# Moving 256 rows of a weight matrix out of the main loads of a one-token attention and gMLP layer

## The chip, the cores and the metric

The kernel runs on one core of one Trainium2 chip. A core has a matrix engine (TensorE, PE in the profile), VectorE (DVE), ScalarE (ACT), GpSimd (POOL) and SyncE (SP), which run their own queues of instructions and wait for each other by semaphores, and 16 DMA engines. The metric is the device time of one execution, in microseconds (us).

## The reference

One token with 576 features is normalised and goes through two branches, whose results are added to it. Branch A is attention over the last 4096 positions of a cache with 16 heads for 32 query heads. Branch B is a gated MLP with 2304 pairs of hidden values.

```python
xn = layernorm(x)                                        # x: [1, 1, 576]
q = (xn @ wq).reshape(1, 1, 32, 128).transpose(0, 2, 1, 3)
k = repeat(k_cache[:, :, 65536 - 4096:, :], 2, axis=1)   # v the same
p = softmax(einsum('bhqd,bhkd->bhqk', q, k) * 128 ** -0.5)
A = einsum('bhqk,bhkd->bhqd', p, v).transpose(0, 2, 1, 3).reshape(1, 1, 4096) @ wo

z = gelu(xn @ w_in)                                      # w_in: [576, 4608]
z1, z2 = z[..., :2304], layernorm(z[..., 2304:])
g = w_sp * z2 + b_sp                                     # one position: two numbers
B = (z1 * g) @ w_out                                     # w_out: [2304, 576]
out = x + A + B
```

All inputs and the output are bfloat16. Some 51 MB are read for one token.

## The kernel before

**Loads.** Nearly all data comes in by DMAs that SyncE issues in a fixed order, near the top of the kernel: wq in two pieces, k blocks 0 and 1, v block 0, then k2, v1, k3, w_in (win), v2, v3, wo in two pieces and w_out (wout) in four. Each fills all 128 partitions of a tile. A block holds four of the 16 cache heads. The tiles come from two pools of two buffers each, "small" and "large", so a load waits until the tile that was in its buffer two turns earlier is used up: wo waits for the z matmuls that read win, and wout for the transposes of k block 3. The scheduler is manual: the program text sets each engine's order, and a framework adds the semaphore waits that its view of the tiles asks for.

**Attention.** For each block b, `turn` (L211) transposes k on VectorE, `scores` (L251) makes the scores on PE and their softmax on VectorE and ScalarE (the exponential p at L279), `weigh` (L287) multiplies by v into pv, which ScalarE copies to pvs (L298), and `heads` (L301) reduces that to eight columns of o_t. `values` is heads after weigh.

**The MLP.** `z_all` (L319) multiplies xn by win on PE (L329), nine steps deep, into two tiles z0 and z1. VectorE copies them into zs (L333 to L336), whose last part GpSimd has set to zero (L321), and transposes zs in 32x32 blocks into zt (L337, L338), so that the hidden values stand on the partitions. `gate` (L341) makes the gelu, the layer norm and the product: a chain of small steps on VectorE with an exponential (L351) and the norm's Ln and Exp (L181, L182) on ScalarE and a sum over the partitions on PE (L362). It ends with hv (L369), the column that multiplies w_out.

**Rows of w_out.** 2304 rows are 18 for each of 128 partitions. In the kernel before, the main load brings 17 rows a partition (FR = 17), rows 128 to 2303. The first 128 rows are the "side rows": two DMAs that ScalarE issues (L382, L383), ahead of its exponential of block 3, bring 96 of them to 12 partitions of eight rows each, and 32 to 32 partitions of one row each. The z values that belong to the side rows are picked from z0 by two small copies (L334, L336), and hv has FC = 26 columns.

**The end.** `row_of` (L392) adds one row of each partition to the result: two matmuls, one for each half of the 576 outputs. PE's order there is: the sum of the gate's layer norm (L362), heads(2), the input row, the side rows, values(3), a transpose of o_t into o_p, 32 rows of wo, and 17 rows of wout; then two copies of the result and two DMAs to the output. The cuts (0, 8, 14, 16, 17) of the main load of w_out let PE begin with its first rows while the rest is on the way.

Of the kernel before, what the change touches and what calls it, by code (L numbers as in the profile page):

```python
# [8 lines left out]
FP32 = mybir.dt.float32  # L9
# [5 lines left out]
P = 128  # L15
D = 576
# [5 lines left out]
FH = 2304  # L22
# [6 lines left out]
NR = 9  # L29
EPS = 1e-5  # L30
SCALE = DH ** -0.5
GELU_C = 0.7978845608028654
FE = P
FR = (FH - FE) // P
FX = 8
FB = 12 * FX
FC = FR + FX + 1
FQ = P * FR // 4
FW = FQ // 2
WR = HQ * DH // P  # L40
HW = D // 2
ZPAD = 24
# [6 lines left out]
def kernel(  # L49
# [14 lines left out]
    nc = tc.nc  # L64
    ctx.enter_context(tc.manual_schedule())

    const = ctx.enter_context(tc.tile_pool(name="const", bufs=1))
    work = ctx.enter_context(tc.tile_pool(name="work", bufs=2))
    one = ctx.enter_context(tc.tile_pool(name="one", bufs=1))
# [7 lines left out]
    ps_a = ctx.enter_context(tc.tile_pool(name="ps_a", bufs=2, space=PS))  # L77


    x_row = const.tile([1, D], BF16, name="x_row")  # L80
    nc.scalar.dma_start(x_row[:], A_x.flatten_outer_dims())
    ws2 = const.tile([1, 2], BF16, name="ws2")
    nc.scalar.dma_start(ws2[:, 0:1], B_w_sp.flatten_outer_dims()[0:1, 0:1])
    nc.scalar.dma_start(ws2[:, 1:2], B_b_sp.flatten_outer_dims()[0:1, 0:1])
# [3 lines left out]
    def unit(name, width):  # L88
        pool = small if width == SMALL else large
        return pool.tile([P, width], BF16, name=name, tag="u")  # L90
# [4 lines left out]
    def load(t, view, width, cuts):  # L95
        for a, e in zip(cuts, cuts[1:]):
            nc.sync.dma_start(t[:, (a - cuts[0]) * width:(e - cuts[0]) * width], view[:, a * width:e * width])
# [19 lines left out]
    win_t = unit("win", LARGE)  # L117
# [3 lines left out]
    wo_t = unit("wo", LARGE)  # L121
    load(wo_t, wo_v, D, (0, 20, WR))
    wout_t = unit("wout", SMALL)
    load(wout_t, B_w_out[FE:FH, :].rearrange("(p r) n -> p (r n)", r=FR), D, (0, 8, 14, 16, FR))


    ident = const.tile([P, P], BF16, name="ident")
# [1 line left out]
    xw = const.tile([P, NR, 32], BF16, name="xw")  # L129
# [91 lines left out]
    for r in range(NR):  # L221
        for g in range(4):
            nc.tensor.matmul(q_ps[32 * g:32 * g + 32, :], lhsT=xw[:, r, :],  # L223
                             rhs=wq_t[:, 2048 * r + 512 * g:2048 * r + 512 * (g + 1)],
                             start=r == 0, stop=r == NR - 1, tile_position=(0, 32 * g))
# [5 lines left out]
    for g in range(4):  # L231
        nc.tensor.matmul(qr[:, :, g, :], lhsT=rep4[:, g, :, :].rearrange("p n q -> p (n q)"),
                         rhs=qT[:, :, 0:2, :].rearrange("p a h e -> p h a e"), start=True, stop=True)
# [17 lines left out]
    def scores(b):  # L251
        sm = one.tile([P, 2, 512], FP32, name=f"sm{b}", tag="sm")
        mx = work.tile([P, 2], FP32, name=f"mx{b}", tag="mx")
        for kk in range(2):
            s_ps = ps_s.tile([P, 512], FP32, name=f"s{b}_{kk}", tag="s")
            for k4 in range(4):
                for ce in range(4):
                    c, e = divmod(ce, 2)
                    nc.tensor.matmul(s_ps[:], lhsT=zq[:, b, ce, ZPAD - 8 * k4:ZPAD - 8 * k4 + P],  # L259
                                     rhs=kt[b, 4 * kk + k4][:, c, :, e],  # L260
                                     start=k4 == 0 and ce == 0, stop=k4 == 3 and ce == 3)
            nc.vector.tensor_tensor_reduce(  # L262
                out=sm[:, kk, :].rearrange("p (n s) -> p n s", s=HB),
                in0=s_ps[:].rearrange("p (n s) -> p n s", s=HB),
                in1=cm[:].unsqueeze(1).to_broadcast([P, P, HB]), scale=SCALE, scalar=-3e38,
                op0=ALU.add, op1=ALU.max, accum_out=mx[:, kk:kk + 1])
        m1 = work.tile([P, 1], FP32, name=f"m1{b}", tag="m1")
        nc.vector.tensor_max(m1[:], mx[:, 0:1], mx[:, 1:2])  # L268
        tr = ps_m.tile([P, P], FP32, name=f"tr{b}", tag="m")
        nc.tensor.matmul(tr[:], lhsT=m1[:].to_broadcast([P, P]), rhs=ident_f[:], start=True, stop=True)  # L270
        m8 = work.tile([P, 8], FP32, name=f"m8{b}", tag="m8")
        nc.vector.tensor_reduce(out=m8[:], in_=tr[:].rearrange("p (a x) -> p x a", x=8), axis=AXX, op=ALU.max)  # L272
        mj = work.tile([P, 8], FP32, name=f"mj{b}", tag="mj")
        nm = work.tile([P, 1], FP32, name=f"nm{b}", tag="nm")
        nc.vector.tensor_tensor_reduce(out=mj[:], in0=m8[:], in1=sel8[:], scale=-1.0, scalar=0.0,  # L275
                                       op0=ALU.mult, op1=ALU.add, accum_out=nm[:])
        p = one.tile([P, 1024], BF16, name=f"p{b}", tag="p")
        l = work.tile([P, 1], FP32, name=f"l{b}", tag="l")
        nc.scalar.activation(p[:], sm[:].rearrange("p k n -> p (k n)"), ACT.Exp, bias=nm[:], accum_out=l[:])  # L279
        p_t[b] = work.tile([P, 2, 16, 32], BF16, name=f"pt{b}", tag="pt")  # L280
        nc.vector.transpose(p_t[b][:].rearrange("p k u m -> p (k u m)"), p[:])  # L281
        su = ps_m.tile([P, 8], FP32, name=f"su{b}", tag="m")
        nc.tensor.matmul(su[:], lhsT=l[:].to_broadcast([P, P]), rhs=sel8[:], start=True, stop=True)  # L283
        rms[b] = work.tile([P, 8], FP32, name=f"rm{b}", tag="rm")
        nc.vector.reciprocal(rms[b][:], su[:])
# [23 lines left out]
    def values(b):  # L309
        heads(b, weigh(b))  # L310


    hv = const.tile([P, FC], BF16, name="hv")

    zt = const.tile([P, FC, 32], FP32, name="zt")
    nc.gpsimd.memset(zt[:, FR:, :], 0.0)


    def z_all():  # L319
        zs = one.tile([P, FQ + 32 * (FX + 1)], FP32, name="zs", tag="sm")  # L320
        nc.gpsimd.memset(zs[0:32, FQ:], 0.0)  # L321
        zx = zs[0:32, FQ:].rearrange("p (r i) -> p r i", i=32)
        zp = [ps_a.tile([P, FE + FW], FP32, name=f"z{i}", tag="a") for i in range(2)]
        for r in range(NR):
            for g in range(4):
                for i in range(2):
                    lead = FE if g == 0 and i == 0 else 0
                    a = FE + FQ * g + FW * i - lead
                    nc.tensor.matmul(zp[i][32 * g:32 * g + 32, FE - lead:], lhsT=xw[:, r, :],  # L329
                                     rhs=win_t[:, FH * r + a:FH * r + a + lead + FW],  # L330
                                     start=r == 0, stop=r == NR - 1, tile_position=(0, 32 * g))
        for i in range(2):
            nc.vector.tensor_copy(zs[:, FW * i:FW * (i + 1)], zp[i][:, FE:])  # L333
        nc.vector.tensor_copy(zx[:, 0:FX, 0:12].rearrange("p r (i x) -> p r i x", x=4),  # L334
                              zp[0][0:32, 0:FB].rearrange("p (x i r) -> p r i x", x=4, i=3))
        nc.vector.tensor_copy(zx[:, FX, :], zp[0][0:32, FB:FE])  # L336
        nc.vector.transpose(zt[:, 0:FR, :], zs[:, 0:FQ].rearrange("p (i r) -> p r i", r=FR))  # L337
        nc.vector.transpose(zt[0:32, FR:, :], zx)  # L338
        return zt[:, :, 0:2]

    def gate(z):  # L341
        def t3(name):
            return const.tile([P, FC, 2], FP32, name=name)

# [8 lines left out]
        nc.vector.reciprocal(e[:], e[:])  # L353
        G = const.tile([P, 2, FC], FP32, name="G")
        nc.vector.tensor_mul(G[:].rearrange("p h c -> p c h"), e[:], z)
        sz = const.tile([P, 2], FP32, name="sz")
        nc.vector.tensor_reduce(out=sz[:, 0:1], in_=G[:, 1, :], axis=AXX, op=ALU.add)
        jz = const.tile([P, FC], FP32, name="jz")
        nc.vector.tensor_tensor_reduce(out=jz[:], in0=G[:, 1, :], in1=G[:, 1, :], scale=1.0, scalar=0.0,
# [3 lines left out]
        mz = rstd_of(sp[:], FH, "mz")  # L363
        gz = const.tile([P, FC], FP32, name="gz")
        nc.vector.tensor_scalar(out=gz[:], in0=G[:, 1, :], scalar1=mz[:, 0:1], scalar2=mz[:, 3:4],
# [12 lines left out]
    values(1)  # L378
    turn(3)

    e0 = D * (FR + FX)
    nc.scalar.dma_start(wout_t[0:12, D * FR:e0], B_w_out[0:FB, :].rearrange("(x i r) n -> i x (r n)", x=4, i=3))  # L382
    nc.scalar.dma_start(wout_t[0:32, e0:e0 + D], B_w_out[FB:FE, :])  # L383
    scores(3)
    z = z_all()
    pvs2 = weigh(2)
    gate(z)
# [4 lines left out]
    def row_of(col, w, start=False, stop=False):  # L392
        for g in range(2):
            nc.tensor.matmul(fin[g][32 * g:32 * g + 1, :], lhsT=col, rhs=w[:, HW * g:HW * (g + 1)],  # L394
                             start=start, stop=stop, tile_position=(0, 32 * g))

    row_of(one_bf[:, 0:1], x_row, start=True)
    for r, rows in [(FR + j, 12) for j in range(FX)] + [(FR + FX, 32)]:
        row_of(hv[0:rows, r:r + 1], wout_t[0:rows, D * r:D * (r + 1)])
    values(3)  # L400


# [48 lines left out]
```

## Time and profile before

| | |
|---|---|
| median of three runs | 127.53 us (127.42 to 127.91) |
| the profiled execution's own time | 127.4 us |
| its span, from the first to the last instruction | 125.6 us |
| mean granted clock of TensorE | 0.864 |
| TensorE busy | 77.5 us (62%) |
| VectorE busy | 64.7 us (52%) |
| ScalarE busy | 10.2 us |
| GpSimd busy | 4.5 us |
| bytes moved by DMA | 51.03 MB, mean 406 GB/s |

Busy times are the time in which the profiler saw an instruction of the engine at work, as a share of the span. In a line of the timeline stand the start, the busy time, the engine, the line of the kernel, the operation, what it writes and reads with shapes, and the number of instructions; in brackets behind it how long the engine had been idle and what ended that. ACTq and SPq are the queues in which ScalarE and SyncE issue DMAs: such a line gives the time of the issue, not of the transfer. The "chain that ended last" follows the work back from the last instruction, at each step to what released it. Durations in ns are of one instruction.

The DMA engines were busy almost throughout: in 40 equal slices of the span their mean busy share was 0.8 or more in all but the first and the last.

### The profile page before, as it was taken

What the parts mean: (1) busy time and instruction counts of PE and PEld (TensorE: products, weight loads), DVE (VectorE), ACT (ScalarE), POOL (GpSimd) and SP (SyncE); (2) the same over time, 40 slices, a digit from 0 to 9 for tenths busy, and PEclk for the clock granted to TensorE, in tenths of its full rate; (3) what the DMA queues carried; (4) which work ended last, traced back from release to release, by engine and by line L of the source; (5) the groups of instructions that cost most, each with busy time, mean ns of one, the idle gap of its engine ahead of it and who ended that gap; (6) DMA issues with size and microseconds to landing.
All of it is one profiled execution on the core that took longest, in us unless ns stands there. A gap on an engine that the chain in (4) does not pass through costs nothing.

```text
span 125.6 us, 1352 instructions
## 1 busy us (share of the span) xinstructions
PE 77.5 (62%) x546; PEld 37.7 (30%) x550; DVE 64.7 (52%) x132; ACT 10.2 (8%) x19; POOL 4.5 (4%) x12
## 2 busy tenths in 40 slices
PE   3230550099922997385799274997397188749661
PEld 3110220033302342225334033342274063235340
DVE  6660032499648998322998445998326840010001
ACT  4010000000021000310000221000300210100001
POOL 8500000000000000000000000000100000000000
PEclk9999999999985599955579999599958975786999
DMA  4999899898998979999898999989898989999960
GB/s 120 506 438 438 365 470 470 365 501 365 470 459 378 485 344 490 407 428 490 355 490 365 508 423 428 423 384 490 358 462 372 487 359 444 448 395 423 396 249 0
DMA packets 2526, 51.03 MB, mean 406 GB/s; under 512 B 298, under 2 KB 461, under 8 KB 717
## 3 DMA queue, kind: packets, MB, share of 16 engines
q1 hardware_dynamic: 2450, 50.81, 94.9%
q10 hardware_dynamic: 71, 0.15, 0.3%
q8 instruction: 4, 0.07, 0.2%
q14 instruction: 1, 0.01, 0.0%
HBM read 50.96 MB, written 0.00 MB: 406 GB/s over the span
## 4 chain that ended last, share of the span: by engine, by line
PE 42%; DMA 37%; DVE 11%; ACT 5%; issue 2%; SPq 1%; ACTq 0%
PE s L259 29%; DMA wout<-in_B_w_out_dram 20%; DMA k<-in_A_k_cache_dram 18%; ACT p L279 4%; PE pv L293 4%; DVE kt L214 4%; PE z L329 4%; PE op L304 2%; DVE sm L262 2%; PE tr L270 2%; PE fin L394 1%; DVE pt L281 1%; DVE m L272 1%; ACT pvs L298 1%; PE su L283 1%
## 5 line engine op out<-in xcount | busy, mean ns | idle before, releaser
L259 PE MATMUL s<-kt,zq 128*128 128x512 bf16 x124 | 36.3, 451 | 11.6 <-DVE kt L214 10.8
L214 DVE STREAM_TRANSPOSE kt<-k 128x1024 f32<-128x1024 f32 x32 | 36.4, 1204 | 3.9 <-DMA k<-in_A_k_cache_dram 3.9
L259 PEld LDWEIGHTS <-zq 128*128 128x128 bf16 x128 | 14.5, 113 | 32.4 <-issue 21.4
L293 PE MATMUL pv<-v,pt 128*32 128x512 bf16 x128 | 10.1, 469 | 1.1 <-DMA v<-in_A_v_cache_dram 1.1
L279 ACT ACTIVATE p<-sm,nm 128x1024 bf16<-128x1024 f32 x4 | 4.6, 1148 | 71.9 <-DVE nm L275 71.9
L223 PE MATMUL q_ps<-wq,xw 128*32 128x512 bf16 x36 | 4.2, 627 | 7.2 <-DMA wq<-in_A_wq_dram 4.9
L307 DVE TENSOR_TENSOR o_t<-op,rm 128x8 bf16<-128x8 f32 x4 | 0.7, 164 | 15.1 <-PE op L304 15.1
L281 DVE STREAM_TRANSPOSE pt<-p 128x1024 bf16<-128x1024 bf16 x4 | 5.0, 1245 | 5.4 <-ACT p L279 5.4
L262 DVE CUSTOM_DVE_ANT_1 sm<-s,cm 128x512 f32<-128x512 f32 x8 | 5.4, 671 | 3.5 <-PE s L259 3.5
L304 PE MATMUL op<-selu,pvs 128*128 128x8 f32 x32 | 5.3, 293 | 2.5 <-ACT pvs L298 2.1
L283 PE MATMUL su<-sel,l 128*128 128x8 f32 x8 | 1.8, 293 | 7.6 <-ACT p L279 7.6
L394 PE MATMUL fin<-wo,o_p 128*1 128x288 bf16 x64 | 5.7, 345 | 1.2 <-DMA wo<-in_A_wo_dram 1.1
L304 PEld LDWEIGHTS op<-selu,pvs 128*128 128x128 f32 x32 | 5.0, 236 | 4.6 <-ACT pvs L298 4.2
L418 DVE CAST res<-fin 1x288 bf16<-1x288 f32 x1 | 0.4, 445 | 11.4 <-PE fin L394 11.4
L394 PE MATMUL fin<-wout,hv 128*1 128x288 bf16 (+2 forms) x52 | 4.8, 336 | 2.3 <-DMA wout<-in_B_w_out_dram 2.2
L293 PEld LDWEIGHTS <-pt 128*32 128x32 bf16 x128 | 3.7, 112 | 5.8 <-issue 3.1
L227 DVE CAST q_sb<-q_ps 128x512 bf16<-128x512 f32 x1 | 0.7, 690 | 8.1 <-PE q_ps L223 8.1
L394 PEld LDWEIGHTS <-o_p 128*1 128x1 bf16 x64 | 3.3, 99 | 4.0 <-issue 1.1
L329 PE MATMUL z<-win,xw 128*32 128x272 bf16 (+1 forms) x72 | 4.4, 396 | 0.0
L270 PE MATMUL tr<-ident_f,m 128*128 128x128 f32 x8 | 2.0, 326 | 3.9 <-DVE m L268 3.9
L223 PEld LDWEIGHTS <-xw 128*32 128x32 bf16 x36 | 1.4, 130 | 9.2 <-issue 9.2
L298 ACT COPY pvs<-pv 128x512 f32<-128x512 f32 x4 | 2.3, 585 | 20.2 <-PE pv L293 20.2
(93 smaller groups left out, 41.8 us busy)
## 6 DMA issues: line engine op xcount, KB each, us to landing
k<-in_A_k_cache_dram SPq DMA_DIRECT2D x4, 4096.0 KB
v<-in_A_v_cache_dram SPq DMA_DIRECT2D x4, 4096.0 KB, 29.2
win<-in_B_w_in_dram SPq DMA_DIRECT2D x1, 5184.0 KB
wq<-in_A_wq_dram SPq DMA_DIRECT2D x1, 3584.0 KB, 12.7
wo<-in_A_wo_dram SPq DMA_DIRECT2D x1, 2880.0 KB
wo<-in_A_wo_dram SPq DMA_DIRECT2D x1, 1728.0 KB, 20.8
wout<-in_B_w_out_dram SPq DMA_DIRECT2D x1, 1152.0 KB
wq<-in_A_wq_dram SPq DMA_DIRECT2D x1, 1024.0 KB, 4.7
```

What stands on the lines that cost most here:

```text
L214: nc.vector.transpose(t[:].rearrange("p c n e -> p (c n e)").bitcast(FP32), kn[b][:, UK * DH * k:UK * DH * (k + 1)].bitcast(FP32).rearrang ...
L223: nc.tensor.matmul(q_ps[32 * g:32 * g + 32, :], lhsT=xw[:, r, :], rhs=wq_t[:, 2048 * r + 512 * g:2048 * r + 512 * (g + 1)], start=r == 0, ...
L259: nc.tensor.matmul(s_ps[:], lhsT=zq[:, b, ce, ZPAD - 8 * k4:ZPAD - 8 * k4 + P], rhs=kt[b, 4 * kk + k4][:, c, :, e], start=k4 == 0 and ce = ...
L262: nc.vector.tensor_tensor_reduce(out=sm[:, kk, :].rearrange("p (n s) -> p n s", s=HB), in0=s_ps[:].rearrange("p (n s) -> p n s", s=HB), in ...
L270: nc.tensor.matmul(tr[:], lhsT=m1[:].to_broadcast([P, P]), rhs=ident_f[:], start=True, stop=True)
L279: nc.scalar.activation(p[:], sm[:].rearrange("p k n -> p (k n)"), ACT.Exp, bias=nm[:], accum_out=l[:])
L281: nc.vector.transpose(p_t[b][:].rearrange("p k u m -> p (k u m)"), p[:])
L293: nc.tensor.matmul(pv[32 * g:32 * g + 32, :].rearrange("p (n d) -> p n d", n=4), lhsT=p_t[b][:, kk, u, :], rhs=v4[:, kk, u, :, :], start=k ...
L298: nc.scalar.copy(pvs[:], pv[:])
L304: nc.tensor.matmul(op[:], lhsT=pvs[:, DH * u:DH * (u + 1)], rhs=selu[:, 8 * u:8 * u + 8], start=u == 0, stop=u == 3)
L329: nc.tensor.matmul(zp[i][32 * g:32 * g + 32, FE - lead:], lhsT=xw[:, r, :], rhs=win_t[:, FH * r + a:FH * r + a + lead + FW], start=r == 0, ...
L394: nc.tensor.matmul(fin[g][32 * g:32 * g + 1, :], lhsT=col, rhs=w[:, HW * g:HW * (g + 1)], start=start, stop=stop, tile_position=(0, 32 * g))
```

## The change

The main load of w_out brings 16 rows a partition instead of 17, in the cuts (0, 8, 13, 15, 16), and 256 rows are side rows. The first 96 of these are brought by ScalarE as before to 12 partitions of eight rows each, but the DMA stands behind scores(3), and so behind the exponential of block 3, in ScalarE's queue. The other 160 are brought by a DMA of GpSimd to the partitions 64 to 79, ten rows each. Ahead of it GpSimd sets the side rows' part of the wout tile to zero (10 columns of rows on 128 partitions), and before and after the block's DMA it issues a small copy, `skip`, of 16 numbers twice for eight and for four partitions, each fourth of the first 32, into columns of the tile that nothing reads. All four stand ahead of the memset of zs on GpSimd.

In z_all the products change shape: per step four of 512 columns into z0, and two, of 96 and 160 columns, into z1, so 54 matmuls instead of 72. zs, zt and hv have 16 + 10 columns. The side rows are ten products over all 128 partitions (the zeros add nothing) instead of nine over 12 or 32. The input row x is loaded in two halves instead of one piece.

```diff
-FE = P
-FR = (FH - FE) // P
-FX = 8
-FB = 12 * FX
-FC = FR + FX + 1
...
+FR = 16
+FA, RA = 96, 8
+FB, RB = 160, 10
+FE = FA + FB
+FC = FR + RB
+FQ = 512
...
-    nc.scalar.dma_start(x_row[:], A_x.flatten_outer_dims())
+    for a in range(0, D, D // 2):
+        nc.scalar.dma_start(x_row[:, a:a + D // 2], A_x.flatten_outer_dims()[:, a:a + D // 2])
...
-    load(wout_t, B_w_out[FE:FH, :].rearrange("(p r) n -> p (r n)", r=FR), D, (0, 8, 14, 16, FR))
+    load(wout_t, B_w_out[FE:FH, :].rearrange("(p r) n -> p (r n)", r=FR), D, (0, 8, 13, 15, FR))
...
-    zt = const.tile([P, FC, 32], FP32, name="zt")
-    nc.gpsimd.memset(zt[:, FR:, :], 0.0)
...
+        zs = one.tile([P, FQ + 32 * RB], FP32, name="zs", tag="sm")
+        nc.gpsimd.memset(zs[:, FQ:], 0.0)
+        zx = zs[:, FQ:].rearrange("p (r i) -> p r i", i=32)
...
         for r in range(NR):
             for g in range(4):
...
+                product(0, g, r, FE + FQ * g, FQ, 0)
+            product(1, 0, r, 0, FA, 0)
+            product(1, 2, r, FA, FB, FA)
+        nc.vector.tensor_copy(zs[:, 0:FQ], zp[0][:])
+        for q, n, a, rows, k in ((0, 12, 0, RA, 3), (64, 16, FA, RB, 4)):
+            nc.vector.tensor_copy(
+                zx[q:q + 32, 0:rows, 0:n].rearrange("p r (i x) -> p r i x", x=4),
+                zp[1][q:q + 32, a:a + n * rows].rearrange("p (x i r) -> p r i x", x=4, i=k))
+        zt = one.tile([P, FC, 32], FP32, name="zt", tag="zt")
         nc.vector.transpose(zt[:, 0:FR, :], zs[:, 0:FQ].rearrange("p (i r) -> p r i", r=FR))
-        nc.vector.transpose(zt[0:32, FR:, :], zx)
+        nc.vector.transpose(zt[:, FR:, :], zx)
...
-    e0 = D * (FR + FX)
-    nc.scalar.dma_start(wout_t[0:12, D * FR:e0], B_w_out[0:FB, :].rearrange("(x i r) n -> i x (r n)", x=4, i=3))
-    nc.scalar.dma_start(wout_t[0:32, e0:e0 + D], B_w_out[FB:FE, :])
+    def blocks(a, e, k):
+        return B_w_out[a:e, :].rearrange("(x i r) n -> i x (r n)", x=4, i=k)
+
+    def skip(k, a):
+        nc.gpsimd.dma_start(wout_t[0:4 * k:4, a:a + 32].rearrange("i (m c) -> i m c", m=2),
+                            B_w_out[0:2 * k, 0:16].rearrange("(m i) n -> i m n", m=2))
+
+    nc.gpsimd.memset(wout_t[:, D * FR:D * FC], 0.0)
+    skip(8, D * FC)
+    nc.gpsimd.dma_start(wout_t[64:80, D * FR:D * FC], blocks(FA, FE, 4))
+    skip(4, D * FC + 32)
     scores(3)
+    nc.scalar.dma_start(wout_t[0:12, D * FR:D * (FR + RA)], blocks(0, FA, 3))
     z = z_all()
...
-    for r, rows in [(FR + j, 12) for j in range(FX)] + [(FR + FX, 32)]:
-        row_of(hv[0:rows, r:r + 1], wout_t[0:rows, D * r:D * (r + 1)])
+    for r in range(FR, FC):
+        row_of(hv[:, r:r + 1], wout_t[:, D * r:D * (r + 1)])
```

In the changed kernel's own line numbers, which the prediction uses for it, skip is L388, GpSimd's memset of wout L391 and its block L393, ScalarE's side rows L396, the memset of zs L318, the copies of the side rows' z L334, their transpose L339, and the gate's sum L363. The other names of lines are those of the kernel before.

More of the change, by code (lines that the diff above doesn't have):

```diff
@@ L32 @@
 GELU_C = 0.7978845608028654
-FE = P
-FR = (FH - FE) // P
-FX = 8
-FB = 12 * FX
-FC = FR + FX + 1
-FQ = P * FR // 4
-FW = FQ // 2
+FR = 16
[4 more added lines that the diff above has]
+FQ = 512
 WR = HQ * DH // P
@@ L313 @@
     hv = const.tile([P, FC], BF16, name="hv")
-    zt = const.tile([P, FC, 32], FP32, name="zt")
-    nc.gpsimd.memset(zt[:, FR:, :], 0.0)
     def z_all():
[L320 to L323, printed above, removed]
+        zs = one.tile([P, FQ + 32 * RB], FP32, name="zs", tag="sm")
+        nc.gpsimd.memset(zs[:, FQ:], 0.0)
@@ L324, in z_all, with product @@
+        zx = zs[:, FQ:].rearrange("p (r i) -> p r i", i=32)
+        zp = [ps_a.tile([P, FQ], FP32, name=f"z{i}", tag="a") for i in range(2)]
+        def product(i, g, r, a, n, to):
+            nc.tensor.matmul(zp[i][32 * g:32 * g + 32, to:to + n], lhsT=xw[:, r, :],
+                             rhs=win_t[:, FH * r + a:FH * r + a + n],
+                             start=r == 0, stop=r == NR - 1, tile_position=(0, 32 * g))
         for r in range(NR):
             for g in range(4):
[L326 to L336, printed above, removed]
+                product(0, g, r, FE + FQ * g, FQ, 0)
+            product(1, 0, r, 0, FA, 0)
+            product(1, 2, r, FA, FB, FA)
+        nc.vector.tensor_copy(zs[:, 0:FQ], zp[0][:])
```

## The prediction

> **What bounds the kernel now.** I read the page first: the share of the engines, the DMA rows and the chain of waits.
>
> ```profile
> span 125.6 us, 1352 instructions
> PE 77.5 (62%) x546; PEld 37.7 (30%) x550; DVE 64.7 (52%) x132; ACT 10.2 (8%) x19; POOL 4.5 (4%) x12
> ...
> q1 hardware_dynamic: 2450, 50.81, 94.9%
> q10 hardware_dynamic: 71, 0.15, 0.3%
> ```
>
> No engine is busy for two thirds of the span, but q1, the queue of SyncE's loads, fills 94.9% of the sixteen DMA engines' time. The stream of loads sets the end, and PE follows it. The timeline of the last 35 us shows how closely, and which instructions the change touches.
>
> ```profile
> 86.12 0.82 ACTq L382 DMA_DIRECT2D wout<-in_B_w_out_dram  x1
> ...
> 90.61 0.33 POOL L321 MEMSET zs<- 32x288 f32 x1 [85.80 <-ACT p L279]
> ...
> 96.12 0.24 DVE L334 COPY zs<-z 32x96 f32<-32x96 f32 x1
> ...
> 96.34 2.55 SPq L97 DMA_DIRECT2D wout<-in_B_w_out_dram  x4
> ...
> 97.90 0.21 DVE L346 TENSOR_TENSOR u<-zt 128x52 f32<-128x52 f32 x1
> ...
> 98.84 0.25 ACT L351 ACTIVATE e<-u 128x52 f32<-128x52 f32 x1 [0.27 <-DVE u L349]
> ...
> 102.71 0.19 DVE L369 TENSOR_TENSOR hv<-G,gz 128x26 bf16<-128x26 f32 x1
> ...
> 102.95 2.31 PE L394 MATMUL fin<-wout,hv 12*1 12x288 bf16 x18
> ...
> 105.69 3.34 PE L293 MATMUL pv<-v,pt 128*32 128x512 bf16 x32 [0.42 <-DMA v<-in_A_v_cache_dram]
> ...
> 112.54 5.78 PE L394 MATMUL fin<-wo,o_p 128*1 128x288 bf16 x64 [1.09 <-DMA wo<-in_A_wo_dram]
> ...
> 119.51 1.15 PE L394 MATMUL fin<-wout,hv 128*1 128x288 bf16 x16 [1.19 <-DMA wout<-in_B_w_out_dram]
> 121.64 1.38 PE L394 MATMUL fin<-wout,hv 128*1 128x288 bf16 x18 [0.98 <-DMA wout<-in_B_w_out_dram]
> ```
>
> GpSimd's memset of zs (90.61) is over long before VectorE needs it (96.12). From there a chain of short steps makes hv (102.90). PE uses hv on the side rows of w_out, then does block 3's values, wo, and w_out. It waits for DMAs at 112.54, 119.51 and 121.64. The work behind hv and ahead of the last w_out rows is long: it fits only because hv is there 18.7 us before the last rows land.
>
> **The change part by part.** The arithmetic moves little. It is the place of three DMAs in GpSimd's queue that decides. The list of the changed program's instructions with their waits has this on GpSimd:
>
> ```
> 13 L391 Memset wout_118 128x5760 [waits DMAHW7_49,DMAHW3_49,DVE_49]
> 14 L388 DMACopy wout_118<-in_B_w_out_dram 8x2x16 [waits DMAHW2_49,DMAHW1_49,Pool_49]
> 15 L393 DMACopy wout_118<-in_B_w_out_dram 16x1x5760
> 16 L388 DMACopy wout_118<-in_B_w_out_dram 4x2x16
> 17 L318 Memset zs_622 128x320 [waits Activation_49]
> ```
>
> The names DMAHW0 to DMAHW7 are semaphores that the DMAs of SyncE and ScalarE take in turn, 16 counts each. The built program's counts for row 14 are 48 on both, the third DMA of each. Counting the DMAs in the program, the third on DMAHW1 is the first piece of w_out (rows 0 to 7 of each partition), and the third on DMAHW2 the second (rows 8 to 12). So the first small copy of skip, which every fourth partition makes look to the framework like an overlap with the main part of wout, waits until these two pieces have landed. In the trace of before that is 119.5 and 121.6 us. Queued behind it on GpSimd are the block of 160 rows, the second skip and the memset of zs. For the memset wait VectorE's copies of z into zs (L334), then the transposes, the gate and hv; for the gate's sums waits PE in the middle of its queue (L363), and behind that stand heads(2), the side rows, values(3), wo and w_out. ScalarE's 96 rows (L396) wait for both skips, and behind them on ScalarE stand the copy of pv2 and the gate's exponential. SyncE waits for none of this: its last loads need only the z matmuls and the transposes of block 3, so there is no deadlock and the loads land as before.
>
> The sum, on the clock of the profiled execution (127.4 us beside a span of 125.6, so 1.8 outside it; the median of the runs is 127.53):
>
> 1. Release. The second piece landed at 121.60. It is one row per partition shorter, 147 KB at 406 GB/s or 0.36 us, and ScalarE's 144 KB are no longer ahead of it, up to as much again on average. I take 121.2.
> 2. Three DMA issues on GpSimd. The trace has none. The issues on the other queues take 0.26 us (the output, ACTq) to 1.17 us (the longest on SPq). I take 1.0 each, between that longest row and L382's 0.82, the row most like them: 3.0 us, bounds 0.8 to 3.5. GpSimd is free at 124.2.
> 3. The memset of zs is 320 wide where before 288 took 0.33: 0.37, to 124.57.
> 4. L334's first copy to u took 1.78 (96.12 to 97.90). Now there are two copies of 0.24 to 0.3 staggered by 0.2, one transpose of 512 columns (1.12 x 512/544 = 1.06) and one of 320 (0.42 for 288 on 32 partitions, 0.66 by the wide one's rate). Some 1.95: u starts at 126.55.
> 5. u to the exponential 0.94 (97.90 to 98.84), exponential to hv 4.06 (98.84 to 102.90): hv at 131.55.
>
> Beside this, ScalarE: the second skip lands 0.8 after its issue (x_row's copy was issued by 1.26 and PE went on at 2.05), then L396's issue 0.82 and the copy of pv 0.58, which with gaps gives 126.4, while the exponential is due at 127.5. It is hidden, with 1.1 us to spare. The Trainium skill, "DMA: Bandwidth & Descriptors", section "Anatomy of one DMA — SWDGE (gpsimd) path", gives a GpSimd DMA a fixed cost of about 2.0 us to its completion. By that estimate, in place of 0.8, ScalarE would be free at 127.66 and the sum 0.16 longer; no run here shows it yet. The 96 rows land about 129 (four packets of 9216 B a DMA engine, 0.35 us each) and the 160 rows before that, both ahead of hv.
>
> 6. From hv to PE's end. The side rows are 20 matmuls instead of 18, at 0.24 us a pair: 2.45. Values(3) has its data: 3.34 in before, 1.9 in blocks 1 and 2 where PE's clock was higher, 2.9 taken. From its end (109.03) to PE's next weights (111.74) it was 2.7, and stays. The wo matmuls no longer wait and take 5.78 as before, or 3.9 at the last pairs' 0.122: 5.0 taken. 32 w_out matmuls at 0.122 a pair, 2.0, and 0.2 for the last to end. Together 15.25: 146.8.
> 7. PE's end to the span's end was 125.6 - 123.02 = 2.6: span 149.4, and with 1.8 outside 151.2 us.
>
> The granted clock is this sum's loosest part. Everything at the slow pace adds 3.1 us (0.45 in values, 2.7 in wo); everything at the fast one takes off 3.3 (1.2, 1.0 and 1.1).
>
> The rest costs nothing at this time scale. GpSimd's new memset of wout (128x5760, by zq's 2.12 us for 2432 some 5.0 us) runs from 86.1 to 91.1 and would have held the zs memset by 0.2 us at the most without the wait. z's 54 matmuls in place of 72 lie behind win. The second half of x_row adds one ScalarE issue of 0.53 us, and q has 5 us of waiting for wq. If that cover were gone it would cost 0.5.
>
> **The rivals.** First, *the wait does not hold*: the semaphores have their 48 counts earlier than I make out, or the list shows a wait that the chip passes. For it speaks that the counts come from a list, not from a run, and that the copy's columns lie behind those of the pieces it waits for; against it, that ScalarE's L382 is listed in before with waits of the same kind (VectorE's count of the last transpose of block 3) and was issued at 86.12, just when that transpose ended (84.89 + 1.20 = 86.09). Then the DMA engines decide. In the trace's packet records, the last piece of w_out lands on eight engines by 121.30, on one at 121.87 and on seven by 122.69: by their counts three that carried ScalarE's rows and four that fetched 16 KB of instructions each. Every engine sheds eight packets of 1152 B (0.35 us) and two of the 32-row copy (0.1); the 160 rows add four packets of 11520 B, 1.74 us, to four engines. If these four are early ones they end at 121.30 + 1.74 - 0.45 = 122.6, the late ones at 122.24: the end moves by 0.1 to 0.45, and the time is 127.2, not slower. The skill's page "DMA: Bandwidth & Descriptors", section "Issuing engines are not separate DMA queues", leaves this case even less: all issuers share the same engines, so the same bytes would take the same 127.4.
>
> Second, *the wait does not hold and a late engine gets the rows*: 122.69 + 1.74 - 0.45 = 124.0, so 128.7. It decides when one of the four is among the seven.
>
> Third, *the wait holds, but only the issue is late and the memset of zs is not behind it* (GpSimd's DMA issues and its memsets in separate queues). Then VectorE goes on as before, but ScalarE's queue still stands at L396 and is free for the exponential at 126.4, as above: hv at 130.5 and the time about 150.1. This lies in the range.
>
> **How the numbers follow.** The wait as in the sum, or the third rival, has 0.95; no wait and even engines 0.03; no wait and a late engine 0.02. The forecast is 151.2. Its range takes the fast clock (-3.3) and the lower bound of the three issues (-2.2) not quite together, and above it the slow clock (+3.1) with issues a little over the longest row: 147.8 to 155.0. About 0.5% (0.64 us) is what a measurement of this kernel can tell from no change. The even engines' 0.45 at most is within that; nothing here gives more. Faster 0.01, same 0.03, slower 0.96.
>
> **What would show it.** In the profile of the changed kernel: GpSimd's zs memset at about 124 in place of 90.6, and its three DMA issues ahead of it after 121; PE idle from about 98 to 128 before the gate's sums; ScalarE's 96 rows issued after the skips; the chain of waits running through DMA wout, GpSimd, VectorE's gate and then PE, with no DMA wait in wo and w_out. The loads' end should be at or a little before 122. I am wrong if the zs memset lies before 96, or if the three issues take several us each.

## The result, and the profile after

The five executions of the changed kernel took 150.82, 151.16, 153.16, 153.52 and 153.81 us, five of the kernel before 127.42 to 127.91. The ratio, 1.184 [1.180, 1.188], compares the two lowest of the changed kernel with the kernel before, and the profiled execution is the one of 153.16. The forecast was 151.2 in a range of 147.8 to 155.0.

The head of the page of the changed kernel:

```profile
span 151.4 us, 1330 instructions
PE 79.0 (52%) x532; PEld 40.0 (26%) x532; DVE 65.1 (43%) x131; ACT 10.1 (7%) x19; POOL 11.1 (7%) x15
...
PE   0334604992599296897449956900000000598793
...
DMA  4999999999999999999898999999999710000000
...
q1 hardware_dynamic: 2450, 50.66, 78.3%
```

SyncE's loads no longer fill the span. The DMA row is high up to the 32nd slice and then almost empty; PE is at zero for eight slices, of which six lie beside the last loads, and does the rest of its work when no data is coming. PE is busy for 79.0 us, as against 77.5, so the 26 us are not work. The waits (engine, line, what ended the wait; us in all, times, longest) say who stood still:

```profile
ACT pvs L298 <- issue: 36.0, 1, 36.0
...
PE sz_ps L363 <- DVE sz L360: 31.6, 1, 31.6
POOL wout L388 <- DMA wout<-in_B_w_out_dram: 29.2, 1, 29.2
DVE zs L334 <- POOL zs L318: 26.6, 1, 26.6
```

Read from the third line up and down: GpSimd's small copy stood for 29.2 us for a load of w_out, VectorE for 26.6 for the memset behind that copy, PE for 31.6 for VectorE, and ScalarE's queue for 36.0. The chain of waits of the changed kernel, from that load on (start, length, what):

```profile
98.09 22.82 DMA wout<-in_B_w_out_dram
...
120.98 0.68 issue
121.66 0.70 POOL wout L388
...
122.94 3.93 DMA wout<-in_B_w_out_dram
...
127.01 0.82 ACTq L396
...
127.93 0.58 ACT pvs L298
```

This goes as forecast up to the third issue and then differently: not through the memset of zs and VectorE, but through the second skip's transfer (3.93 us from the start of its issue) and ScalarE's queue. The timeline of the same stretch has both paths:

```profile
123.51 0.38 POOL L318 MEMSET zs<- 128x320 f32 x1
123.93 0.58 DVE L334 COPY zs<-z 32x96 f32<-32x96 f32 x2 [26.60 <-POOL zs L318]
...
126.00 0.21 DVE L347 TENSOR_TENSOR u<-zt 128x52 f32<-128x52 f32 x1
...
128.41 0.25 ACT L352 ACTIVATE e<-u 128x52 f32<-128x52 f32 x1
...
132.49 0.18 DVE L370 TENSOR_TENSOR hv<-G,gz 128x26 bf16<-128x26 f32 x1
...
141.10 5.67 PE L406 MATMUL fin<-wo,o_p 128*1 128x288 bf16 x64 [0.28 <-DVE o_p L420]
```

u starts at 126.00 and the exponential would follow 0.94 later by the kernel before, at 126.94; it starts at 128.41, when ScalarE has issued its 96 rows and copied pv. VectorE's path alone would have been 1.47 us earlier. No matmul of wo or w_out waits for a DMA any more: the rows had been there for 19 us and more.

### The profile page after: what moved, and what is told of

It reads as the page before. It is cut to its first block, busy times and chain, and to the rows that moved or that the text cites. A ratio compares the mean times of both kernels' runs of the same rounds, so it can differ in the third digit from the quotient of the medians.

```text
span 151.4 us, 1330 instructions
## 1 busy us (share of the span) xinstructions
PE 79.0 (52%) x532; PEld 40.0 (26%) x532; DVE 65.1 (43%) x131; ACT 10.1 (7%) x19; POOL 11.1 (7%) x15
## 4 chain that ended last, share of the span: by engine, by line
PE 47%; DMA 32%; DVE 9%; ACT 4%; issue 3%; SPq 1%; POOL 1%; ACTq 1%; POOLq 0%
PE s L259 25%; DMA wout<-in_B_w_out_dram 18%; DMA k<-in_A_k_cache_dram 14%; PE fin L406 7%; PE pv L293 6%; PE op L304 4%; DVE kt L214 3%; PE z L323 3%; ACT p L279 3%; DVE sm L262 2%; ACT pvs L298 2%; PE tr L270 1%; SPq L97 1%; PE su L283 1%; DVE pt L281 1%
## 5 line engine op out<-in xcount | busy, mean ns | idle before, releaser
L259 PE MATMUL s<-kt,zq 128*128 128x512 bf16 x128 | 37.5, 461 | 11.1 <-DVE kt L214 11.1
L363 PE MATMUL sz_ps<-sz,ones_f 128*128 128x2 f32 x2 | 0.6, 362 | 31.6 <-DVE sz L360 31.6
L334 DVE COPY zs<-z 32x96 f32<-32x96 f32 (+1 forms) x2 | 0.6, 284 | 26.6 <-POOL zs L318 26.6
L293 PE MATMUL pv<-v,pt 128*32 128x512 bf16 x128 | 12.0, 498 | 0.0
L391 POOL MEMSET wout<- 128x5760 bf16 x1 | 4.9, 4897 | 83.0 <-DVE kt L214 83.0
L363 PEld LDWEIGHTS sz_ps<-sz,ones_f 128*128 128x128 f32 x2 | 0.5, 310 | 32.1 <-DVE sz L360 32.1
L293 PEld LDWEIGHTS <-pt 128*32 128x32 bf16 x128 | 5.6, 120 | 3.8 <-issue 2.6
L406 PE MATMUL fin<-wout,hv 128*1 128x288 bf16 x52 | 4.7, 346 | 0.0
L323 PE MATMUL z<-win,xw 128*32 128x512 bf16 (+2 forms) x54 | 4.4, 448 | 0.0
L161 PE MATMUL x_ps<-one_bf,x_row 1*64 1x1 bf16 x9 | 1.2, 248 | 5.6 <-DMA x_row<-in_A_x_dram 5.6
```

The source lines that it names most:

```text
L293: nc.tensor.matmul(pv[32 * g:32 * g + 32, :].rearrange("p (n d) -> p n d", n=4), lhsT=p_t[b][:, kk, u, :], rhs=v4[:, kk, u, :, :], start=k ...
L323: nc.tensor.matmul(zp[i][32 * g:32 * g + 32, to:to + n], lhsT=xw[:, r, :], rhs=win_t[:, FH * r + a:FH * r + a + n], start=r == 0, stop=r = ...
L391: nc.gpsimd.memset(wout_t[:, D * FR:D * FC], 0.0)
```

## The experiments

Theory: the strided write of skip makes its DMA wait for two pieces of w_out, and what stands behind it on GpSimd, VectorE and ScalarE stands too. Rivals: the rows or their place cost the time without any wait (more side rows, a late DMA engine); or only one of the two things behind the wait, the memset of zs or ScalarE's rows, carries it.

**Is it the stride?** The same two copies, to adjacent partitions in place of every fourth. Rows, order and bytes stay.

```diff
-        nc.gpsimd.dma_start(wout_t[0:4 * k:4, a:a + 32]...
+        nc.gpsimd.dma_start(wout_t[0:k, a:a + 32]...
```

> Both skips write eight and four adjacent partitions instead of each fourth one; everything else is as in the changed kernel, and the two waits of 48 counts are gone from GpSimd's list. If the wait is the cause: the zs memset lies before 96 again, hv is ready by 105, the stream of loads sets the end, and the time is 126.9 to 127.6. If GpSimd's DMAs themselves, or the new shapes (memset of wout, ten side rows over 128 partitions), cost the time: above 140. If the block of 160 rows meets a late DMA engine: about 128.7.

In this kernel's trace GpSimd waits for no load any more, and the time is 127.31 us (127.19 to 127.41), 0.997 [0.996, 0.998] of the kernel before. The timeline of this kernel:

```profile
92.89 0.70 POOL L388 DMA_DIRECT2D wout<-in_B_w_out_dram  x1
...
93.59 0.59 POOL L393 DMA_DIRECT2D wout<-in_B_w_out_dram  x1
...
106.53 2.08 PE L406 MATMUL fin<-wout,hv 128*1 128x288 bf16 x16 [2.09 <-DMA wout<-in_B_w_out_dram]
...
121.54 1.36 PE L406 MATMUL fin<-wout,hv 128*1 128x288 bf16 x16 [0.48 <-DMA wout<-in_B_w_out_dram]
```

GpSimd's three issues follow its memset at once, and the memset of zs is over by 95.13. The block lands late enough for PE to wait 2.09 us at 106.53, which the wait for the last loads at 121.54 swallows. So two copies of 768 bytes in all, for nothing but the partitions that they name, cost 24 to 26 us, and everything else in the change is worth a third of a per cent of gain.

**Does the wait do it alone?** The kernel before, with one strided copy of this kind behind ScalarE's side rows and nothing else of the change.

```diff
     nc.scalar.dma_start(wout_t[0:32, e0:e0 + D], B_w_out[FB:FE, :])
+    nc.gpsimd.dma_start(wout_t[0:32:4, D * FC:D * FC + 32]..., B_w_out[0:16, 0:16]...)
     scores(3)
```

> The kernel before with one small copy of skip added on GpSimd, behind ScalarE's side rows in the text and ahead of the zs memset. If the wait is the cause: released at 121.6, issue 0.70, memset 0.33, then 1.78 + 0.94 + 4.06 to hv at 129.4, 15.9 from there to PE's end, 4.4 to the time's end: 149.8. If the time lies in the new shapes or in the 160 rows' DMA: 127.5, as before.

152.38 us (151.75 to 152.97), ratio 1.194 [1.190, 1.198]. From the timeline of this kernel:

```profile
122.56 0.69 POOL L384 DMA_DIRECT2D wout<-in_B_w_out_dram  x1 [117.73 <-DMA wout<-in_B_w_out_dram]
123.24 0.36 POOL L321 MEMSET zs<- 32x288 f32 x1
```

One added DMA, whose data nobody reads, makes the kernel before as slow as the changed one. The median is 2.6 us over what I had expected, the profiled execution (152.97) 3.2. Of that 1.2 us lie ahead of hv (130.58, not 129.4), most of it because the issue came 0.8 us after the landing, and 2.1 behind hv (17.96 to PE's end, not 15.9), where the clock was low (below). That it is just as slow as the changed kernel is in part chance: its hv is 2.1 us earlier than the changed kernel's.

**Which of the two queues?** First, only the memset of zs behind the wait: ScalarE's rows go ahead of the skips.

```diff
-    skip(8, D * FC)
+    scores(3)
+    nc.scalar.dma_start(wout_t[0:12, D * FR:D * (FR + RA)], blocks(0, FA, 3))
+    skip(8, D * FC)
     nc.gpsimd.dma_start(wout_t[64:80, D * FR:D * FC], blocks(FA, FE, 4))
     skip(4, D * FC + 32)
-    scores(3)
-    nc.scalar.dma_start(...)
```

> The changed kernel with ScalarE's 96 rows ahead of the skips in the text, so that ScalarE waits for nothing of GpSimd; the zs memset is still behind the skips and the block. Theory of two queues: the exponential is then due when u is, at 126.9 instead of 128.4, so the changed kernel's time less 1.5: 149 to 152. Rival, that ScalarE's wait is the whole cost: about 127.5.

Then the other way: block and memset of zs ahead, then the skips, then ScalarE's rows.

```diff
-    skip(8, D * FC)
     nc.gpsimd.dma_start(wout_t[64:80, D * FR:D * FC], blocks(FA, FE, 4))
-    skip(4, D * FC + 32)
     scores(3)
-    nc.scalar.dma_start(...)
     z = z_all()
+    skip(8, D * FC)
+    skip(4, D * FC + 32)
+    nc.scalar.dma_start(wout_t[0:12, D * FR:D * (FR + RA)], blocks(0, FA, 3))
```

> The changed kernel with the block's DMA and the zs memset ahead of both skips on GpSimd; ScalarE's 96 rows still wait for the skips. Theory of two queues side by side: VectorE's chain is free, but ScalarE stands: skips issued by 122.9, landed 124.1, issue 0.82, copy of pv 0.6, exponential at 125.5, which is 2.9 earlier than in the changed kernel, so its time less 2.9: 148 to 150.5. Rival, that the memset behind the skips is the whole cost: about 127.5.

The first took 150.88 us (149.48 to 152.32), the second 153.69 (152.6 to 154.18). Timeline of the first:

```profile
91.70 0.82 ACTq L393 DMA_DIRECT2D wout<-in_B_w_out_dram  x1
...
127.36 0.25 ACT L352 ACTIVATE e<-u 128x52 f32<-128x52 f32 x1 [28.74 <-DVE u L350]
```

and of the second:

```profile
92.65 0.38 POOL L318 MEMSET zs<- 128x320 f32 x1
...
124.76 1.12 POOL L388 DMA_DIRECT2D wout<-in_B_w_out_dram  x2 [31.72 <-DMA wout<-in_B_w_out_dram]
...
128.56 0.25 ACT L352 ACTIVATE e<-u 128x52 f32<-128x52 f32 x1
```

In the first ScalarE is free and waits for VectorE; in the second the memset of zs is out of the way at 93.03 and VectorE's u starts at 98.53, and the exponential still starts at 128.56, behind ScalarE's copy of pv. Either path carries the whole delay: that it is only the one or only the other is wrong. The two shortest executions of the first (149.48 and 149.82) are 1.3 us below those of the changed kernel (150.82 and 151.16), near the 1.5 that I had expected. The second run is over what I expected of it by some 3 us. Its release is late: the second piece of w_out landed at 124.12, 3.2 us after that of the changed kernel (120.91). What moved is the block: it is issued at 91.93 and not after the release, and the skip on eight partitions no longer precedes it. But the delay is not only that of the four DMA engines that carry the block: even the first of the sixteen had its part of the piece 2.2 us later (121.36, not 119.19). The run with the skips last, below, has the same order and shows where that comes from.

**Nothing behind the wait, and what the skips move.** Block, ScalarE's rows and z_all first, the strided skips last.

```diff
-    skip(8, D * FC)
     nc.gpsimd.dma_start(wout_t[64:80, D * FR:D * FC], blocks(FA, FE, 4))
-    skip(4, D * FC + 32)
     ...
     z = z_all()
+    skip(8, D * FC)
+    skip(4, D * FC + 32)
```

> The changed kernel's skips, still to each fourth partition and still waiting for the two pieces of w_out, but moved behind the block's DMA, ScalarE's 96 rows and the zs memset, so that nothing waits behind them. If queueing behind the wait is the whole cost, the 25 us are gone although the wait is still there: below 131. If the skips cost by themselves: above 140. Where it lies below 131 tells of the block's place: if GpSimd's DMA takes the next four engines in turn, the block now goes to the engines that carry ScalarE's rows, as in the run with only ScalarE behind the skips, where the second piece landed at 124.1: the loads end about 125.4, PE 0.4 later, and the time is 130. If the block's place does not matter: 127.3.

130.24 us (130.10 to 130.47), ratio 1.020 [1.019, 1.022]. Its timeline:

```profile
124.57 1.35 PE L406 MATMUL fin<-wout,hv 128*1 128x288 bf16 x16 [0.60 <-DMA wout<-in_B_w_out_dram]
125.15 1.12 POOL L388 DMA_DIRECT2D wout<-in_B_w_out_dram  x2 [30.86 <-DMA wout<-in_B_w_out_dram]
```

The skips wait for 30.86 us and nobody waits for them: 21 to 23 us of the loss are gone with the wait still there. The other 2.9 us over the kernel with adjacent skips (127.31) come from the loads, whose end is 3.0 us later (125.60, not 122.57). They have two parts.

The smaller one is balance. The last piece landed on twelve DMA engines by 124.22 and on four between 125.17 and 125.60. The block runs as four rows of four packets, so on four engines; here three of these rows begin just where a packet of ScalarE's rows ends (97.41, 97.63 and 97.74), so three engines carry both. With the skip on eight partitions ahead of it the block lies elsewhere. From the first to the last engine the end is now spread over 3.2 us in place of 2.1, which is 1.2 us of the 3.0. This is the second rival's mechanism.

The larger one is common to all sixteen engines: the first of them ends 1.9 us later too (122.37, not 120.51). From 97 to 106 us, while the block's packets are on the way, the engines are as busy as with adjacent skips but move less. The same stretch (window, length, busy times with instructions, granted clock, DMA share, GB/s), with adjacent skips and with the skips last:

```profile
97.00:106.00 9.00, 3.71 (x43) 2.69 (x35) 5.94 (x22) 1.33 (x4) 0.00 (x0) 0.88 1.00 424
...
97.00:106.00 9.00, 3.67 (x43) 2.64 (x34) 5.94 (x22) 1.33 (x4) 0.00 (x0) 0.88 1.03 347
```

In the packet records nearly all of v's packets of 32 KB take 1.3 to 1.95 us in this stretch, where they take 1.22 with adjacent skips. The run with only ScalarE behind the skips has the same (341 GB/s), and there ScalarE's rows come over 30 us later, so it is not their meeting with the block. Why the loads slow down when the block is GpSimd's first DMA stays open.

**The block behind both skips.** To see why the second skip took 3.9 us, the block was moved behind it.

```diff
     skip(8, D * FC)
-    nc.gpsimd.dma_start(wout_t[64:80, D * FR:D * FC], blocks(FA, FE, 4))
     skip(4, D * FC + 32)
+    nc.gpsimd.dma_start(wout_t[64:80, D * FR:D * FC], blocks(FA, FE, 4))
```

> The changed kernel with the block of 160 rows issued behind both skips instead of between them. If the second skip landed late (126.87, 3.4 us after its issue had ended) because its packets stood behind the block's on four DMA engines: it lands about 124.2 now, ScalarE's 96 rows are issued by 124.5 instead of 127.0, and the exponential waits for u alone and lies near 127.0 instead of 128.4; the time 1 to 2 us below the changed kernel's in a like run. If a GpSimd DMA simply takes 3 us or more to land: ScalarE's issue stays near 126.5.

One execution, 149.49 us. The view of DMAs from 120 to 130 us gives each issue with its size and the time from the start of the issue to the landing. In the changed kernel it has, for the two skips:

```profile
wout<-in_B_w_out_dram POOLq DMA_DIRECT2D x1, 0.5 KB, 1.9
wout<-in_B_w_out_dram POOLq DMA_DIRECT2D x1, 0.2 KB, 3.9
```

In this one:

```profile
wout<-in_B_w_out_dram POOLq DMA_DIRECT2D x1, 0.5 KB, 1.8
wout<-in_B_w_out_dram POOLq DMA_DIRECT2D x1, 0.2 KB, 1.7
```

The small copy of 0.2 KB lands after 1.7 us when only the other small one is ahead of it, and after 3.9 behind the block's packets. By the landing records of the changed kernel, twelve of its sixteen parts were there by 124.66 and four at 126.66 to 126.87, each some 0.2 us behind one of the last four parts of the block (126.48 to 126.70). In the run with the block behind:

```profile
124.43 0.81 ACTq L396 DMA_DIRECT2D wout<-in_B_w_out_dram  x1
...
127.16 0.25 ACT L352 ACTIVATE e<-u 128x52 f32<-128x52 f32 x1 [1.23 <-DVE u L350]
```

ScalarE's rows are issued at 124.43 and not at 127.01, the exponential waits for VectorE again, and hv is done at 131.42, 1.25 earlier than in the changed kernel.

**The clock behind hv.** One more execution of the changed kernel took 154.03 us, a little over what I expected of it; the release (121.12) and the stretch from hv to PE's end (16.56) came as expected.

> The changed kernel once more, for a second look at its profile: 150.8 to 153.8, second piece of w_out landed between 120.9 and 122, hv 11 us behind that, and 15 to 18 us from hv to PE's end, by when PE's clock comes up.

From the end of hv to the end of PE's work there are 160 matmuls in each of these kernels. Their windows, each from a view of its own (window, length, busy times with instructions, granted clock, DMA share, GB/s): the block behind the skips,

```profile
131.42:145.08 13.66, 12.17 (x160) 7.66 (x160) 0.74 (x4) 0.59 (x1) 0.00 (x0) 0.88 0.00 1
```

the changed kernel (in its second profile 16.56 us at 0.72),

```profile
132.67:148.73 16.06, 14.58 (x160) 8.54 (x160) 0.74 (x5) 0.58 (x1) 0.00 (x0) 0.74 0.00 1
```

and the kernel before with one strided copy:

```profile
130.58:148.54 17.96, 16.48 (x160) 9.01 (x160) 0.74 (x4) 0.59 (x1) 0.00 (x0) 0.61 0.00 1
```

No data comes in these stretches (DMA share 0.00), and their length follows the clock: 13.66 us at 0.88, 17.96 at 0.61 (in the last some of the 160 matmuls have other shapes). The half clock that began 3 to 5 us into PE's idle time ended at 134.64, 137.56, 138.77 and 144.58 in these four profiles (in the order 0.88, 0.74, 0.72, 0.61), 3 to 14 us after hv. In both profiles of the changed kernel a second stretch of half clock followed, from 140.97 to 144.39 and from 142.19 to 145.60, over most of wo: its matmuls took 5.67 us in the first of them and 4.08 at the full clock of the run with the block behind the skips. What sets these moments stays open; between two profiles of the same kernel the end of the first stretch moved by 1.2 us. Whether this makes the spread of the changed kernel's five executions (3.0 us) is not shown: their mean clocks, 0.805 and 0.771 in the two shortest and 0.785 to 0.809 in the others, do not order them.

**Can the version with adjacent skips be bettered?** In it PE waited 2.09 us for the block's rows. There the side rows were put behind values(3).

```diff
-    for r in range(FR, FC):
-        row_of(hv[:, r:r + 1], ...)
     values(3)
+    for r in range(FR, FC):
+        row_of(hv[:, r:r + 1], ...)
```

> The kernel with skips to adjacent partitions, and the side rows of w_out behind values(3) instead of ahead: PE no longer waits 2.1 us for GpSimd's block at 106.5. If the end is set by the last landing of w_out: 127.3, no change. If PE's chain is the bound (it had 0.5 us of waiting left ahead of the second piece): faster by up to 0.3 us.

127.26 us (127.13 to 127.47), against 127.31 without the move: no difference, because PE still waits until 121.53 for the second piece of w_out (landed at 121.49), and the last piece lands at 122.55. Both beat the kernel before by 0.3% (ratio here 0.997 [0.996, 0.998]).

## Why the prediction was right, step by step

The sum gave 149.4 of span, the profile has 151.4. Step by step:

| step | forecast | measured |
|---|---|---|
| 1. second piece landed | 121.2 | 120.9 |
| 2. GpSimd's three issues | 3.0, at once | 1.85, after 0.75 |
| 3. memset of zs ends | 124.57 | 123.89 |
| 4. u starts | 126.55 | 126.00 |
| beside it: ScalarE free for the exponential | 126.4 | 128.4 |
| 5. exponential; end of hv | 127.5; 131.55 | 128.41; 132.67 |
| 6. hv to PE's end | 15.25 | 16.06 |
| 7. to the span's end | 2.6 | 2.67 |

**Right: the wait, and who stands behind it.** The release came where the counts of the list put it, within 0.3 us. The first rival, that the wait does not hold, is refuted by the 29.2 us of the waits; the price that it named, 127.2, is what the kernel with adjacent skips showed (127.31). Its sum had the loads' end at 122.6, and in that kernel it was 122.57. Beside it stood the rule of the Trainium skill, "DMA: Bandwidth & Descriptors", section "Issuing engines are not separate DMA queues", from which I worked out that the same bytes would take the same time. The block's rows and ScalarE's do meet on the same engines, as it says and as the packets of the run with the skips last show, but the time was 0.3% less with adjacent skips and 2% more with the skips last. The second rival's mechanism is real in that run, but it had the loads' end at 124.0 and not at 125.60: it was a sum of balance alone, and did not have the slower packets of all sixteen engines.

**Mis-sized: step 2.** The issues take 0.57 to 0.70 us on GpSimd, not 1.0; the nearest rows, on the other queues, were too long. The 0.75 us between the landing (120.91) and the first issue (121.66) was not in the sum. Together 2.60 against 3.0.

**Wrong: "It is hidden, with 1.1 us to spare."** This is the step that failed. ScalarE was the last to be ready for the exponential, by 1.47 us. I took 0.8 us from a lone load of x_row for the second skip's landing and did not see that the same DMA engines had just been given the block: by the landing at 126.87 it took 3.4 us from the end of its issue (123.51). The run with the block behind the skips shows the cause: 1.25 us of hv come back. The Trainium skill, "DMA: Bandwidth & Descriptors", section "Anatomy of one DMA — SWDGE (gpsimd) path", gives a fixed cost of about 2.0 us for such a DMA; the traces come near it with 1.7 to 1.9, counted from the start of the issue and with nothing ahead on the engines. By that figure, as an estimate, the skip lands at 124.9 to 125.5 and ScalarE is free at 126.5 to 127.1 (the landing and 1.54 us, as measured), not at 128.4: the packets ahead of it decided, not the fixed cost.

**The third rival** (the memset is not behind the wait) is refuted in the changed kernel, where the memset follows the third issue directly. Where an experiment took the memset out from behind the wait, ScalarE's path alone kept the time, as the rival said, but at 153.69 and not 150.1, since the release was later there.

**Step 6** is 0.8 us over: from hv to the end of values(3) 5.71 (5.35 forecast), from there to wo 2.72 (2.7), wo until w_out begins 5.51 (5.0), w_out 2.12 (2.2). The clock was the loosest part as said; in wo it was the second stretch of half clock. Measured, hv to PE's end went from 13.66 to 17.96 in the four profiles, within the bounds of -3.3 and +3.1 about 15.25. That the total came near the forecast is in part luck: the short issues (-0.4 with the gap) and the earlier release (-0.3) made up for a part of ScalarE's path and step 6. The profiled execution is 2.0 us over the sum; the two shortest (150.82 and 151.16), beside the forecast of 151.2, have no profile that shows their steps.

**Not on any path, but not as forecast:** the second half of x_row landed at 5.46 us, just after wq's first piece (5.34), where the whole row had landed by 2.0 in the kernel before. It held PE for 5.6 us, in time that q waits for wq in any case: the second part of q's matmuls starts at 13.88 here and at 13.99 in the kernel before. The 18.7 us that the prediction counts from hv to the last rows are those to the second piece (121.60); the last piece landed at 122.69.

## What to carry to other kernels

Look up in the built program what a small DMA waits for: a destination with a stride over partitions can be taken for an overlap with loads that it never touches, and then the wait falls on everything behind it in that queue, here 24 to 26 us for 768 bytes. Put what nobody needs last in its queue: in the run with the skips last that took 21 to 23 us off. Then look at the loads again, for the new order of GpSimd's DMAs cost 2.9 us there. When a transfer is called hidden, count the packets that the same DMA engines were given just before it.

## What the runs showed of the hardware

A DMA of GpSimd takes 0.57 to 0.73 us of its queue, and 0.6 to 0.8 us go by between the last landing that it waits for and its issue. Whether two tiny copies that nothing reads stood ahead of the block or last was worth 2.9 us (127.31 against 130.24): 1.2 by the engines that the block then shared with ScalarE's rows, the rest because all sixteen engines moved less for some 9 us (347 GB/s, not 424), for a reason that stays open. After some 30 us of idleness, PE worked at half clock for 3 to 14 us beyond hv in the four profiles; for the same 160 matmuls that makes 13.66 to 16.56 us from hv to PE's end, and 17.96 for those of the kernel before with one strided copy.
